# A planned attention and mixture kernel: the order of all queues made anew with other durations

## The chip, the cores and the metric

The kernel runs on one core of a Trainium2 chip. The metric is the device time of one execution in microseconds (us); the time of a kernel is the median of its runs. The core has five engines that run queues of their own, each in its written order: TensorE (PE; PEld is its weight load), VectorE (DVE), ScalarE (ACT), GpSimd (POOL) and SyncE (SP), which here only issues transfers. An engine waits for another by semaphores.

## What is computed

An attention whose scores are cut at a threshold below the row's maximum, and behind it a soft mixture of experts over the 4608 tokens of the attention's output.

```python
batch, n_heads, seq, head_dim = (8, 8, 576, 64)          # attention
N, D, E, S_per_e, F = (4608, 512, 8, 4, 1024)            # mixture
...
scores = scale * np.matmul(q, k.transpose(0, 1, 3, 2))
thresh = np.max(scores, axis=-1, keepdims=True) - tau
scores = np.where(scores >= thresh, scores, -1000000000.0)
attn = np.exp(scores - max); attn = attn / (sum + 1e-09)
x = np.matmul(attn, v)                                   # tokens x 512
...
logits = x @ phi                                         # 32 slots
d = softmax of logits over the tokens; slot_input = d.T @ x
h = np.maximum(slot_input[e] @ w1[e], 0.0); slot_out[e] = h @ w2[e]
c = softmax of logits over the slots; out = c @ slot_out
```

## The kernel before

**The attention stage** works on 32 pairs of heads, four for each of eight batches. A pair has nine score tiles of 128 queries by 576 keys: four blocks of 128 queries for each head, and one tile with the 64 leftover queries of both. For each tile TensorE multiplies q and k (L603, the leftover tile L608) into one of four PSUM regions. VectorE negates and copies the scores to a buffer `ss` (one of four) and takes their maximum in the same instruction (L615, followed by a short read of its accumulator). ScalarE makes exponentials of `ss` (L625). GpSimd adds tau to the maximum, a threshold of 128 numbers (L628). VectorE masks the exponentials by comparing `ss` with the threshold, and sums each row (L631). TensorE transposes the masked tiles into PSUM (L514), and ScalarE drains these to `pTa` and `pTb` (L519). TensorE multiplies them with V (L724), again into PSUM, and ScalarE drains that to `xT`.

The row sums go their own way: GpSimd adds a small number to the nine (L654), VectorE inverts them (L656), TensorE transposes them (L660), ScalarE drains them (L663), and SP writes them to device memory and reads them back spread over 64 rows each, as `R` (L666, L668, L671). Then GpSimd multiplies `xT` by `R` (L735). GpSimd also scales the next pair's keys (L567). After four pairs a **batch** ends: the logits (L796), exponentials with sums (L810), and the weighted sum of the tokens (L854, L859), which VectorE adds up in `acc` (L866).

**The tail** runs the experts: the weights that were not loaded during the attention stage, 38 transfers of 512 KB, stream in as buffers come free (L494, L496), TensorE multiplies them (L1055, L1092), and at last each token's mixture is computed and written out (L1136 to L1154).

**The order.** `pair` and `dispatch` do not issue work, they record operations in the list `G` (`Order.add`): engine, planned duration in ns, a nominal place, what is read and written. `Order.plan` then plays the list through with these durations, engine by engine: an engine takes the first of its next eight operations, by nominal place, whose inputs have come and whose buffers are free. The nominal places are numbers of the table `TABLE`, one for each operation of a pair, of a batch, and of the first and last ones. `LAT`, `CROSS` and `SAME` are what the plan adds between an operation and one that needs it; `more` corrects that for transfers. VectorE's masking instruction is marked `port=True`, and the plan lengthens it by 0.4 of the time for which GpSimd is still busy. What the plan starts first is written first, so the plan sets each queue's order, but only the chip sets the times.

Of the kernel before, what the change touches and what calls it, by code (L numbers as in the profile page):

```python
# [20 lines left out]
SAME = {"PE": 0, "DVE": 127, "ACT": 143, "POOL": 0, "SP": 2100}  # L21
# [19 lines left out]
for _n, _v in (  # L41
    ("batch", [
        20.265, 14.265, 22.458, 9.009, 14.083, 17.552, 21.280, 18.242, 23.399, 15.876, 23.639, 23.042, 19.525, 25.170,
        24.800, 22.578, 20.491,
    ]),
    ("end", [
        422.116, 101.628, 414.958, 444.428, 399.691, 457.508, 321.760, 634.874, 20.930, 417.720, 326.651, 574.203, 281.359,
        409.111, 490.768, 521.489, 539.548, 449.024, 949.190, 840.896, 21.300, 23.130, 583.989, 164.080, 735.574, 648.733,
        100.559, 245.423, 250.790, 679.817, 606.604, 75.253, 282.537,
    ]),  # L50
    ("first", [
# [8 lines left out]
    ]),  # L60
    ("head", [
        -486.655, -149.150, -116.459, -124.700, -355.836, -124.560, -124.240, -390.508, -284.773,
    ]),
    ("last", [
# [6 lines left out]
    ]),  # L71
    ("new0", [
        15.072, 8.053, 29.690, 11.400, 11.400, 11.500, 11.500, 18.149,
    ]),
    ("new1", [
        0.767, 12.245, 29.710, 11.400, 11.400, 11.500, 11.500, 22.125,
    ]),
    ("new2", [
        0.909, 15.170, 28.520, 11.400, 11.400, 11.500, 11.500, 16.909,
    ]),  # L80
    ("new3", [
        13.266, 9.302, 27.910, 11.400, 11.400, 11.500, 11.500, 7.214,
# [32 lines left out]
    ]),  # L115
    ("soft", [
        271.203, 288.777, 241.601, 224.162, 194.540, 428.743,
    ]),
    ("sums", [
        19.392, 21.213, 16.986, 20.521,  # L120
# [243 lines left out]
def softmax_attention_soft_moe(  # L364
# [17 lines left out]
    nc = tc.nc  # L382
# [84 lines left out]
    G = Order(kinds)  # L467
# [14 lines left out]
    n = NPRE + NHOST  # L482
# [752 lines left out]
```

## Time and profile before

| what | us |
|---|---|
| median of 3 runs (lowest to highest) | 540.19 (537.8 to 540.97) |
| the profiled execution, its own time | 539.73 |
| span of the profile | 537.6 |
| TensorE busy, share of the span | 517.3, 96% |
| VectorE busy | 472.0, 88% |
| ScalarE busy | 436.7, 81% |
| GpSimd busy | 243.2, 45% |

A page of the profile gives busy times over the whole span. They mix the attention stage, to about 460 us, with the tail. A view by stretches separates the two, and a timeline has the start and the duration of each instruction; a row with a count joins instructions that follow each other. In the timeline one score multiplication is four records of TensorE. The ends of matmuls are modelled and overlap the next ones, so the distance from one start to the next tells more than a duration. In brackets stands how long the engine was idle before, and what ended it.

### The profile page before, as it was taken

How to read it: one execution, taken by the hardware profiler on the slowest of the kernel's cores; microseconds unless marked ns; L12 is line 12 of the kernel's file. 1: busy time of each engine (PE TensorE's matmuls, PEld its weight loads, DVE VectorE, ACT ScalarE, POOL GpSimd, SP SyncE). 2: the span in 40 equal slices, each digit the busy share in tenths (PEclk: the TensorE clock that was granted, in tenths of full speed). 3: DMA queues.
4: the chain of work that ended last, by engine and by line, in shares of the span. 5: the costliest groups of instructions: out<-in, count | busy, mean ns of one | idle time of the engine just before them, and what ended most of it. 6: DMA issues, size and time to landing. Idle time of an engine off the chain costs nothing. (4 is left out here: it accounts for less than half of the span.)

```text
span 537.6 us, 18151 instructions
## 1 busy us (share of the span) xinstructions
PE 517.3 (96%) x6886; PEld 345.8 (64%) x6886; DVE 472.0 (88%) x1307; ACT 436.7 (81%) x784; POOL 243.2 (45%) x413
## 2 busy tenths in 40 slices
PE   8999999999999999999999999999999999999890
PEld 6566666676676676766766667766766766643370
DVE  6999999999999999999999999999999999613192
ACT  3898998988998899889989999989988999611181
POOL 2544564366535464545444643655346635021030
PEclk9999999999999999999999999999999999999996
DMA  6467676667556654544334444443344332999498
GB/s 156 99 192 192 195 192 194 190 182 193 166 152 193 184 165 154 127 110 98 113 93 115 115 114 115 114 116 114 111 118 116 103 106 104 389 409 408 161 382 321
DMA packets 37890, 92.31 MB, mean 172 GB/s; under 512 B 6068, under 2 KB 15020, under 8 KB 37804
## 3 DMA queue, kind: packets, MB, share of 16 engines
q1 hardware_dynamic: 37484, 90.90, 55.5%
q8 instruction: 54, 0.88, 0.7%
q10 hardware_dynamic: 320, 0.26, 0.2%
q14 instruction: 32, 0.26, 0.2%
HBM read 81.56 MB, written 9.58 MB: 170 GB/s over the span
## 5 line engine op out<-in xcount | busy, mean ns | idle before, releaser
L628 POOL TENSOR_SCALAR small<-small 128x1 f32<-128x1 f32 x288 | 143.0, 502 | 199.4 <-DVE ss L615 183.0
L615 DVE TENSOR_SCALAR_CACHE_REDUCE ss<-ps 128x576 f32<-128x576 f32 x288 | 208.9, 752 | 6.8 <-issue 2.3
L631 DVE SCALAR_TENSOR_TENSOR p<-ss,small,p 128x576 f32<-128x576 f32 x256 | 206.1, 825 | 0.9 <-POOL small L628 0.3
L625 ACT ACTIVATE p<-ss,small 128x576 f32<-128x576 f32 x256 | 186.5, 775 | 9.6 <-DVE ss L615 8.4
L603 PE MATMUL ps<-k,q 64*128 64x288 f32 x1024 | 159.0, 423 | 1.0 <-POOL small L628 0.9
L603 PEld LDWEIGHTS ps<-k,q 64*128 64x128 f32 x1024 | 85.7, 188 | 21.4 <-DVE ss L615 3.4
L514 PE MATMUL ps<-ident,p 64*128 64x64 f32 x2304 | 95.5, 224 | 0.6 <-ACT pTb L519 0.2
L514 PEld LDWEIGHTS ps<-ident,p 64*128 64x128 f32 x2304 | 86.3, 138 | 13.0 <-DVE ss L615 1.3
L519 ACT COPY pTb<-ps 128x1024 f32<-128x1024 f32 (+1 forms) x96 | 82.8, 874 | 10.9 <-PE ps L514 10.4
L724 PE MATMUL ps<-pTb,vv 128*64 128x320 f32 x512 | 76.0, 439 | 0.0
L519 ACT COPY pTa<-ps 128x1024 f32<-128x1024 f32 x64 | 63.1, 1011 | 0.8 <-PE ps L514 0.5
L724 PE MATMUL ps<-pTa,vv 128*64 128x256 f32 x512 | 62.3, 385 | 0.1
L724 PEld LDWEIGHTS ps<-pTb,vv 128*64 128x64 f32 x512 | 33.9, 136 | 34.1 <-ACT pTb L519 3.2
L735 POOL TENSOR_TENSOR xT<-xT,R 128x576 f32<-128x576 f32 x31 | 50.1, 1615 | 10.1 <-DMA R<-rd 4.2
L724 PEld LDWEIGHTS ps<-pTa,vv 128*64 128x64 f32 x512 | 33.9, 136 | 21.9 <-ACT pTa L519 3.6
L519 ACT COPY xT<-ps 128x256 f32<-128x256 f32 (+1 forms) x62 | 24.7, 398 | 5.8 <-PE ps L724 5.8
L631 DVE SCALAR_TENSOR_TENSOR pL<-ss,small,pL 128x576 f32<-128x576 f32 x32 | 28.4, 887 | 0.0
L625 ACT ACTIVATE pL<-ss,small 128x576 f32<-128x576 f32 x32 | 25.2, 787 | 3.1 <-DVE ss L615 3.1
L1012 POOL TENSOR_TENSOR c<-lall,crow 128x512 f32<-128x512 f32 x9 | 9.3, 1044 | 37.7 <-PE ct L506 23.4
L654 POOL TENSOR_SCALAR small<-small 128x9 f32<-128x9 f32 x31 | 16.7, 538 | 15.2 <-DVE p L631 8.1
L567 POOL TENSOR_SCALAR k<-k,small 128x576 f32<-128x576 f32 x31 | 23.4, 754 | 0.0
L615 DVE DVE_READ_ACCUMULATOR ss<-ps 128x1 f32 x288 | 23.4, 81 | 0.0
(159 smaller groups left out, 528.3 us busy)
## 6 DMA issues: line engine op xcount, KB each, us to landing
w<-in_w SPq DMA_DIRECT2D x45, 512.0 KB
q<-in_qT SPq DMA_DIRECT2D x62, 288.0 KB
vv<-in_vt SPq DMA_DIRECT2D x32, 320.0 KB
host<-in_w SPq DMA_DIRECT2D x19, 512.0 KB
k<-in_kT SPq DMA_DIRECT2D x62, 144.0 KB
R<-rd SPq DMA_DIRECT2D x62, 144.0 KB
out<-host SPq DMA_DIRECT2D x9, 512.0 KB
out<-w SPq DMA_DIRECT2D x7, 512.0 KB
```

Source lines behind the costliest of these rows:

```text
L514: nc.tensor.transpose(out=s[:, g, c:c + 64], in_=ins[g], identity=ident[rows[g], rows[g]], tile_position=(64 * g, 0))
L519: G.add("ACT", 51 + 0.833 * n, nom, lambda: nc.scalar.copy(*io()), r, w)
L567: scaled = lambda e, c=slice(0, S): lambda: e.tensor_scalar(out=kt.t[:, c], in0=kt.t[:, c], scalar1=flag8, **one)
L603: nc.tensor.matmul(s.t[:, g, 0:HS], qt.t[rows[g], h, c * 128:(c + 1) * 128], kt.t[rows[g], h * HS:(h + 1) * HS], start=True, stop=True, ti ...
L615: dve(674, t + OFF['mx'], [s], [ss, nmx], lambda s=s, ss=ss, nmx=nmx: nc.vector.tensor_scalar(out=ss.t.rearrange("p (a k) -> p a k", a=2), ...
L625: G.add("ACT", 668, t + OFF['ex'], lambda sv=sv, nmx=nmx, view=view: nc.scalar.activation(view().rearrange("p (a k) -> p a k", a=2), sv(), ...
L628: pool(250, t + OFF['th'], lambda nmx=nmx, thr=thr: nc.gpsimd.tensor_scalar(out=thr.t, in0=nmx.t, scalar1=1.0, scalar2=pabs, op0=ALU.mult, ...
L631: fn=lambda sv=sv, thr=thr, view=view, at=at: nc.vector.scalar_tensor_tensor(out=view().rearrange("p (a k) -> p a k", a=2), in0=sv(), scal ...
L654: pool(292, t + OFF['ri'], lambda: nc.gpsimd.tensor_scalar(out=ri.t[:, 0:N9], in0=r.t, scalar1=1e-9, scalar2=1.0, op0=ALU.add, op1=ALU.mul ...
L724: nc.tensor.matmul(W.t[h * 64:(h + 1) * 64, a, o:o + p0.shape[-1]], vv.t[:, v0:v0 + 64], p0, start=(kb == 0), stop=(kb == 4), tile_positio ...
L735: G.add("POOL", 1140, u + 5.6, own=own, r=[R], w=[xT], fn=lambda: nc.gpsimd.tensor_tensor(out=xT.t, in0=xT.t, in1=R.t, op=ALU.mult))
L1012: nc.gpsimd.tensor_tensor(out=c4, in0=lall[:, rows].unsqueeze(2).to_broadcast([128, k, 4, NS]), in1=crow[:, rows].unsqueeze(2).unsqueeze(3 ...
```

## The change

No operation is added or removed. Six planned durations or waits are other numbers: GpSimd's multiplication (L735) 1460 ns for 1140; ScalarE's two exponentials with sums 450 and 370 for 260 and 207; SP's three writes of the row sums 310, 450 and 620 for 600 each; its two reads back 550 for 650, with `more` -1000 for -1500; and what the plan adds between two operations of SP that depend on each other, 3300 for 2100. All numbers of the table but a few are new. The 0.4 for the port stays.

```diff
-SAME = {"PE": 0, "DVE": 127, "ACT": 143, "POOL": 0, "SP": 2100}
+SAME = {"PE": 0, "DVE": 127, "ACT": 143, "POOL": 0, "SP": 3300}
...
     ("batch", [
-        20.265, 14.265, 22.458, 9.009, 14.083, 17.552, 21.280, 18.242, 23.399, 15.876, 23.639, 23.042, 19.525, 25.170,
...
+        18.302, 10.858, 22.929, 20.593, 20.846, 23.057, 21.280, 21.310, 24.957, 22.816, 22.335, 22.234, 21.154, 25.170,
...
     ("sums", [
-        19.392, 21.213, 16.986, 20.521,
+        22.198, 17.464, 28.328, 56.205,
...
                 G.add("ACT", 158, t + 3.3, own=own, r=[w], w=[rt], fn=lambda w=w: nc.scalar.copy(
                     rt.t[0:N9].rearrange("p (g q) -> p g q", g=2), w.t[0:N9, :, 0:64]))
                 for h in range(2):
-                    G.add("SP", 600, t + 3.4, own=own, r=[rt], w=[rd[0, h]], more=-2500, fn=lambda h=h: nc.sync.dma_start(
+                    G.add("SP", 310 + 140 * h, t + 3.4, own=own, r=[rt], w=[rd[0, h]], more=-2500, fn=lambda h=h: nc.sync.dma_start(
                         rd.t[h, 0:SM].rearrange("(c q) -> c q", c=4), rt.t[h * 4:h * 4 + 4]))
-                G.add("SP", 600, t + 3.4, own=own, r=[rt], w=[rd[1]], more=-2500, fn=lambda: nc.sync.dma_start(
+                G.add("SP", 620, t + 3.4, own=own, r=[rt], w=[rd[1]], more=-2500, fn=lambda: nc.sync.dma_start(
                     rd.t[:, SM:S].unsqueeze(0), rt.t[8:9].rearrange("o (h q) -> o h q", h=2)))
                 for g in range(2):
-                    G.add("SP", 650, t + 3.5, own=own, r=[rd], w=[R[g]], more=-1500, fn=lambda g=g: nc.sync.dma_start(
+                    G.add("SP", 550, t + 3.5, own=own, r=[rd], w=[R[g]], more=-1000, fn=lambda g=g: nc.sync.dma_start(
                         R.t[rows[g]], rd.t[g:g + 1].to_broadcast([64, S])))
             elif not late and h == 1:
                 G.skip(4)
 ...
-            G.add("POOL", 1140, u + 5.6, own=own, r=[R], w=[xT], fn=lambda: nc.gpsimd.tensor_tensor(
+            G.add("POOL", 1460, u + 5.6, own=own, r=[R], w=[xT], fn=lambda: nc.gpsimd.tensor_tensor(
                 out=xT.t, in0=xT.t, in1=R.t, op=ALU.mult))
...
-        for k, (o, n) in enumerate(((slice(0, 128), 260), (slice(128, 192), 207))):
+        for k, (o, n) in enumerate(((slice(0, 128), 450), (slice(128, 192), 370))):
             G.add("ACT", n, u + 1.6, own=sums, r=[wl, new["run"]], w=[d["exp"], PERS["dsum"]], fn=lambda o=o, k=k: nc.scalar.activation(
                 d.t[:, o], lone(wl)[:, o], AF.Exp, bias=new.t[:, 1:2], accum_out=dsum[:, k:k + 1]))
```

What the table does is seen in the built program. TensorE, around the first scores of a new pair (here keys `k_239`), behind the attention-times-V of the pair before; `p` are masked tiles, `ps` are PSUM regions. Before:

```order
L514 MATMUL ps_256<-ident,p_219 128x64 x2
L514 MATMUL ps_256<-ident,p_199 128x64 x2
L514 MATMUL ps_257<-ident,p_199 128x64 x16
L603 MATMUL ps_258<-k_239,q_243 128x288 x2
L603 MATMUL ps_255<-k_239,q_243 128x288 x2
L514 MATMUL ps_256<-ident,p_215 128x64 x16
L514 MATMUL ps_257<-ident,p_203 128x64 x16
L608 MATMUL ps_258<-k_239,q_243 64x288 x4
L603 MATMUL ps_255<-k_239,q_243 128x288 x2
L603 MATMUL ps_256<-k_239,q_243 128x288 x2
```

After:

```order
L514 MATMUL ps_256<-ident,p_219 128x64 x2
L514 MATMUL ps_256<-ident,p_199 128x64 x2
L514 MATMUL ps_255<-ident,p_203 128x64 x16
L603 MATMUL ps_257<-k_239,q_243 128x288 x2
L603 MATMUL ps_256<-k_239,q_243 128x288 x2
L603 MATMUL ps_258<-k_239,q_243 128x288 x2
L603 MATMUL ps_255<-k_239,q_243 128x288 x2
L514 MATMUL ps_257<-ident,pL_171 128x64 x10
```

Two runs of two scores with transposes and the leftover tile (L608) between became one run of four, over all four regions; the leftover tile stands later.

VectorE, some rows into the second pair of the third batch; `ss0` to `ss3` are the four score buffers. Before:

```order
L615 TENSOR_SCALAR ss0_183,small_68<-ps3_258 128x576
L631 SCALAR_TENSOR_TENSOR p21_199,small_68<-ss1_211,small_68,p21_199 128x576
L615 TENSOR_SCALAR ss1_211,small_68<-ps2_257 128x576
L631 SCALAR_TENSOR_TENSOR p22_215,small_68<-ss2_207,small_68,p22_215 128x576
L615 TENSOR_SCALAR ss2_207,small_68<-ps1_256 128x576
L631 SCALAR_TENSOR_TENSOR p23_203,small_68<-ss1_211,small_68,p23_203 128x576
```

After:

```order
L631 SCALAR_TENSOR_TENSOR p21_199,small_68<-ss3_187,small_68,p21_199 128x576
L615 TENSOR_SCALAR ss0_207,small_68<-ps1_256 128x576
L615 TENSOR_SCALAR ss3_187,small_68<-ps0_255 128x576
L631 SCALAR_TENSOR_TENSOR p23_211,small_68<-ss2_163,small_68,p23_211 128x576
L615 TENSOR_SCALAR ss2_163,small_68<-ps1_256 128x576
L631 SCALAR_TENSOR_TENSOR p22_203,small_68<-ss0_207,small_68,p22_203 128x576
```

Before, two L615 here write the buffer that the L631 just ahead has read (`ss1`, `ss2`); after, one does (`ss2`).

VectorE, at the end of that batch's first pair. Before:

```order
L631 SCALAR_TENSOR_TENSOR p22_215,small_68<-ss0_183,small_68,p22_215 128x576
L631 SCALAR_TENSOR_TENSOR p22_215,small_68<-ss3_163,small_68,p22_215 128x576
L615 TENSOR_SCALAR ss0_183,small_68<-ps2_257 128x576
L631 SCALAR_TENSOR_TENSOR p23_203,small_68<-ss2_207,small_68,p23_203 128x576
L631 SCALAR_TENSOR_TENSOR p23_203,small_68<-ss1_211,small_68,p23_203 128x576
```

After:

```order
L631 SCALAR_TENSOR_TENSOR p22_203,small_68<-ss0_207,small_68,p22_203 128x576
L631 SCALAR_TENSOR_TENSOR p23_211,small_68<-ss1_215,small_68,p23_211 128x576
L631 SCALAR_TENSOR_TENSOR p22_203,small_68<-ss2_163,small_68,p22_203 128x576
L631 SCALAR_TENSOR_TENSOR pL0_171,small_68<-ss3_187,small_68,pL0_171 128x576
L615 TENSOR_SCALAR ss0_207,small_68<-ps0_255 128x576
```

Four L631 now stand in a row. Such rows of four were one in the whole program and are nine.

## Rows read from the trace of the kernel before

**Rows 1.** The page: busy us, share of the span, instructions of each engine.

```profile
PE 517.3 (96%) x6886; PEld 345.8 (64%) x6886; DVE 472.0 (88%) x1307; ACT 436.7 (81%) x784; POOL 243.2 (45%) x413
```

**Rows 2.** By stretch: length, busy us of PE, PEld, DVE, ACT, POOL, clock, DMA.

```profile
20.00:60.00 40.00, 39.46 (x534) 26.93 (x534) 39.55 (x112) 35.98 (x61) 19.89 (x35) 1.00 0.59 164
...
240.00:300.00 60.00, 59.86 (x850) 41.46 (x848) 58.19 (x163) 54.08 (x99) 30.23 (x51) 1.00 0.45 115
```

**Rows 3.** Timeline of TensorE in the second batch: start us, duration us, what, records.

```profile
101.51 0.83 PE L514 MATMUL ps<-ident,p 64*128 64x64 f32 x20
102.18 1.67 PE L603 MATMUL ps<-k,q 64*128 64x288 f32 x12
103.69 0.47 PE L514 MATMUL ps<-ident,pL 64*128 64x64 f32 x10
...
108.43 0.66 PE L514 MATMUL ps<-ident,p 64*128 64x64 f32 x16
108.92 1.19 PE L603 MATMUL ps<-k,q 64*128 64x288 f32 x8
109.95 0.66 PE L514 MATMUL ps<-ident,p 64*128 64x64 f32 x16
110.54 1.84 PE L724 MATMUL ps<-pTb,vv 128*64 128x320 f32 x12
```

**Rows 4.** Timeline of TensorE: the logits of batches 2, 3, 4 and 8.

```profile
86.41 1.53 PE L796 MATMUL ps<-xT,phi_sb 128*32 128x128 f32 x64
142.84 1.53 PE L796 MATMUL ps<-xT,phi_sb 128*32 128x128 f32 x64
200.66 1.53 PE L796 MATMUL ps<-xT,phi_sb 128*32 128x128 f32 x64
...
427.81 1.53 PE L796 MATMUL ps<-xT,phi_sb 128*32 128x128 f32 x64
```

**Rows 5.** Timeline of VectorE: an L615 behind an L631 of the same buffer.

```profile
98.39 0.08 DVE L631 DVE_READ_ACCUMULATOR pL<-ss,small,pL 128x1 f32 x1
98.59 0.76 DVE L615 TENSOR_SCALAR_CACHE_REDUCE ss<-ps 128x576 f32<-128x576 f32 x1
99.27 0.08 DVE L615 DVE_READ_ACCUMULATOR ss<-ps 128x1 f32 x1
99.27 0.82 DVE L631 SCALAR_TENSOR_TENSOR p<-ss,small,p 128x576 f32<-128x576 f32 x1
```

**Rows 6.** Timeline of several engines at three places where GpSimd and an L631 meet.

```profile
109.60 1.14 DVE L631 SCALAR_TENSOR_TENSOR p<-ss,small,p 128x576 f32<-128x576 f32 x1
...
173.38 2.05 DVE L631 SCALAR_TENSOR_TENSOR pL<-ss,small,pL 128x576 f32<-128x576 f32 x1
173.42 1.40 POOL L735 TENSOR_TENSOR xT<-xT,R 128x576 f32<-128x576 f32 x1 [0.20 <-DMA R<-rd]
...
175.59 0.52 PE L514 MATMUL ps<-ident,pL 64*128 64x64 f32 x10 [0.76 <-DVE pL L631]
...
441.69 1.24 POOL L567 TENSOR_SCALAR k<-k,small 128x576 f32<-128x576 f32 x1
...
442.24 1.29 DVE L631 SCALAR_TENSOR_TENSOR p<-ss,small,p 128x576 f32<-128x576 f32 x1
```

**Rows 7.** Timeline of TensorE: a run of four scores, and what follows it.

```profile
443.12 2.46 PE L603 MATMUL ps<-k,q 64*128 64x288 f32 x16
...
445.40 0.47 PE L514 MATMUL ps<-ident,pL 64*128 64x64 f32 x10
```

**Rows 8.** One source line: count, ns least/median/most, first and last start.

```profile
L735 POOL TENSOR_TENSOR xT<-xT,R x31: 1402/1458/1938, 32.1 to 456.1; 128x576 f32<-128x576 f32 x31
```

**Rows 9.** Timeline near the beginning: the second pair's keys and its first scores.

```profile
15.31 0.73 POOL L567 TENSOR_SCALAR k<-k,small 128x576 f32<-128x576 f32 x1
...
16.80 0.60 PE L603 MATMUL ps<-k,q 64*128 64x288 f32 x2 [0.90 <-POOL small L628]
```

**Rows 10.** By stretch, as rows 2: the tail while weights load.

```profile
464.00:503.00 39.00, 38.57 (x448) 16.96 (x446) 9.79 (x35) 7.67 (x22) 5.63 (x21) 1.00 1.01 401
```

More of the change, by code (lines that the diff above doesn't have):

```diff
@@ L42 @@
     ("batch", [
-        20.265, 14.265, 22.458, 9.009, 14.083, 17.552, 21.280, 18.242, 23.399, 15.876, 23.639, 23.042, 19.525, 25.170,
-        24.800, 22.578, 20.491,
+        18.302, 10.858, 22.929, 20.593, 20.846, 23.057, 21.280, 21.310, 24.957, 22.816, 22.335, 22.234, 21.154, 25.170,
+        24.800, 26.493, 25.629,
     ]),
     ("end", [
-        422.116, 101.628, 414.958, 444.428, 399.691, 457.508, 321.760, 634.874, 20.930, 417.720, 326.651, 574.203, 281.359,
-        409.111, 490.768, 521.489, 539.548, 449.024, 949.190, 840.896, 21.300, 23.130, 583.989, 164.080, 735.574, 648.733,
@@ L49 @@
-        100.559, 245.423, 250.790, 679.817, 606.604, 75.253, 282.537,
+        301.862, 124.881, 561.835, 326.908, 282.443, 488.775, 203.147, 786.750, 20.930, 629.636, 84.039, 874.559, 430.695,
+        399.561, 811.773, 370.590, 728.139, 341.016, 1042.783, 587.554, 21.300, 23.130, 823.228, 97.206, 1287.503, 1073.630,
+        374.223, 289.576, 665.706, 1244.037, 1191.015, 400.282, 474.095,
     ]),
     ("first", [
[8 rows of a table removed]
[8 rows of a table added]
     ]),
     ("head", [
-        -486.655, -149.150, -116.459, -124.700, -355.836, -124.560, -124.240, -390.508, -284.773,
+        -467.603, -149.150, -24.974, -124.700, -435.660, -124.560, -124.240, -804.214, -510.213,
@@ L63 @@
     ]),
     ("last", [
[6 rows of a table removed]
[6 rows of a table added]
     ]),
     ("new0", [
-        15.072, 8.053, 29.690, 11.400, 11.400, 11.500, 11.500, 18.149,
+        -2.119, 9.625, 29.690, 11.400, 11.400, 11.500, 11.500, 14.554,
     ]),
     ("new1", [
-        0.767, 12.245, 29.710, 11.400, 11.400, 11.500, 11.500, 22.125,
+        8.351, 13.344, 29.710, 11.400, 11.400, 11.500, 11.500, 9.243,
     ]),
     ("new2", [
-        0.909, 15.170, 28.520, 11.400, 11.400, 11.500, 11.500, 16.909,
+        16.352, 12.163, 28.520, 11.400, 11.400, 11.500, 11.500, 0.814,
@@ L80 @@
     ]),
     ("new3", [
-        13.266, 9.302, 27.910, 11.400, 11.400, 11.500, 11.500, 7.214,
+        7.519, 11.154, 27.910, 11.400, 11.400, 11.500, 11.500, 4.909,
     ]),
     ("pair0", [
[6 rows of a table removed]
[6 rows of a table added]
     ]),
     ("pair1", [
[6 rows of a table removed]
[6 rows of a table added]
     ]),
     ("pair2", [
[6 rows of a table removed]
[6 rows of a table added]
     ]),
     ("pair3", [
[6 rows of a table removed]
[6 rows of a table added]
     ]),
     ("soft", [
-        271.203, 288.777, 241.601, 224.162, 194.540, 428.743,
+        317.283, 270.993, 516.784, 155.887, 694.551, 783.864,
     ]),
     ("sums", [
-        19.392, 21.213, 16.986, 20.521,
+        22.198, 17.464, 28.328, 56.205,
@@ L121 @@
     ]),
     ("sumsend", [
-        192.259, 178.027, 591.492, 458.793,
+        586.760, 390.095, 532.994, 498.283,
     ]),
```

76 rows, old and new, of the table TABLE are left out of this document.

## The prediction

> **What bounds the kernel now.** I read the page's busy times first, then the busy times by stretch, then the timeline of TensorE. The page gives TensorE 96% of the span and VectorE 88% [rows 1]. The stretches tell more: from 20 to 60 us VectorE is busy 39.55 of 40 us, and later it is busy 58.19 of 60 with TensorE at 59.86 and the granted clock at 1.00 throughout [rows 2]. So two queues are full at once. TensorE's busy time proves little by itself, since matmuls overlap; the distances between starts prove more. Two score multiplications (x8 in the timeline) take 1.03 us to the next start and three (x12) take 1.51, so one costs 0.48 and a run of them 0.06 on top. A transpose of 16 records takes 0.49 before a score run and 0.59 before an attention-times-V block, so leaving the form that scores and transposes share costs 0.10. A transpose of 20 right after such a block takes 0.67 where 20/16 of 0.49 is 0.61, so coming back costs 0.06 [rows 3]. The starts recur at just these distances nearly everywhere: TensorE issues without a pause, and its time is set by how much work it has and how often it changes form. The pace shows in the start of the logits (L796), one a batch: 56.43 us to the next, then 57.82, then four batches in 227.15, or 56.79 each [rows 4].
>
> After the last attention work the weights are the limit: from 464 to 503 us the DMA engines are busy over their whole time [rows 10]. The queue of SP around them stays as it is: the row sums of the last pair but one, their spreading, then the loads. A main stage that is shorter by some time starts them sooner by that time, and the end moves with them.
>
> **The change, part by part.** No instruction is added or removed in the main stage; the planner gets other durations and a new table, and so all queues stand in another order. I price what can be counted.
>
> *TensorE's changes of form.* Counted over the attention stage, the runs of score multiplications go from 142 to 138, the exits from that shared form from 88 to 80 (leftover scores now often stand right before an attention-times-V block), and the returns from 86 to 78. With the prices above: 4 x 0.06 + 8 x 0.10 + 8 x 0.06 = 1.5 us less. This lies on TensorE's own queue, which nothing covers; I take it whole.
>
> *GpSimd's multiplication, planned at 1.46 us instead of 1.14.* The trace has it 31 times, 1.402, 1.458 and 1.938 us long (least, median, most) [rows 8]. What it does to VectorE is plain: while it runs, a masking instruction (L631, 0.81 us elsewhere) that falls due does not finish: 1.14 us at 109.60, and 2.05 at 173.38, where the multiplication took 1.40 from 173.42 [rows 6]. At 173.38 TensorE then stood still 0.76 us for that result [rows 6]; this is the batch that took 57.82 instead of 56.79, so 1.03 lost. It is not part of the pattern that repeats from batch to batch, but came where GpSimd ran off its plan. With the measured duration in the plan I take it away: 1.0 us. The bounds are 0 (another takes its place) and, on top of the 1.0, all that the batches lose against the shortest one: 8 x (56.79 - 56.43) = 2.9.
>
> The Trainium skill ("SBUF — State Buffer", section "Who interferes with whom") has this as an exclusive lock of a shared port pair: whoever starts first holds it for its whole instruction. The rows at 173 agree (0.81 + 1.24 = 2.05, of 1.40). It speaks against the change, since the planner, after it as before, charges VectorE only 0.4 of the overlap: by the 0.4 the new places of (b) below would cost 0.4 x 5.7 = 2.3 us, by the lock, as the rows have it, 5.7.
>
> *VectorE's queue.* Three things move. (a) A maximum instruction (L615) that stands right behind the L631 that read the same buffer waits for that to drain: it starts 0.20 us after the L631's last part began, 98.39 to 98.59, where otherwise the next starts at once [rows 5]. There are 29 such places before and 16 after: 13 x 0.20 = 2.6 us less. (b) In the written order, 7 of the 31 multiplications stand where one L615 and then an L631 follow (the 1.14 us case, 0.33 too long); after it are 14: 7 x 0.33 = 2.3 more. The scaling of the keys (L567) stands between L631 in a row once before, at 441.69, where L631 took 1.29 at 442.24 [rows 6], and 8 times after: 1.29 - 0.81 = 0.48, so 7 x 0.48 = 3.4 more, 5.7 together. (c) The stray stall at 173.38, 2.05 - 0.81 = 1.2, goes. Sum: -2.6 + 5.7 - 1.2 = +1.9 us. The bounds are -2.6 - 1.2 = -3.8 (the new places do not collide) and +3.1 (the stray stays). VectorE gains no room, so TensorE's gain can be used only as far as VectorE keeps up; most of these stalls did not reach TensorE before, whose starts stayed regular [rows 3], so I count none of them in the forecast.
>
> *Longer runs of scores.* Runs of four go from 2 to 23. The fourth needs the fourth PSUM region, which ScalarE must have drained; the run at 443.12, behind that stalled L631, is the only one in the steady stage of before. It took 2.28 us to the next start where 0.06 + 4 x 0.48 = 1.98 were due [rows 7]: 0.30 lost. A run of three shows no loss [rows 3]. In the new order the drain of that region stands, in two places of three, right behind two short drains with no exponential between them, so I take 0 (nearest to the run of three) and keep 0.30 each as the other bound.
>
> *The beginning.* TensorE idles 0.90 us at 16.80 until GpSimd has scaled the next keys (15.31) [rows 9]. In the new order that scaling stands one L628 earlier. But VectorE is full from there to 60 us [rows 2], so the gain is between 0 and 0.9; I take 0.
>
> *Small transfers and exponentials with sums.* Their new durations only move others; their instructions are the same and none ends a wait on TensorE in the rows. The transfers of row sums are planned nearer to each other on SP; they gate GpSimd's multiplication alone. I take 0. At the end the last multiplication stands behind the last L628 as before, and the last L631 behind both, so I take no change there.
>
> **Sum.** 1.5 + 1.0 = 2.5 us less. The profiled execution took 539.73 us, 0.46 below the median of 540.19 of three; from the median I forecast 540.2 - 2.5 = **537.7 us**. A measurement of this kernel can tell about 0.5%, 2.7 us, from no change.
>
> **Rivals.** *All waits of TensorE go.* Besides the 2.5: 2.9 for the batches and 0.9 at the beginning, together 6.3: 533.9 us. For it: the repeating waits are short and the plan now has their causes right. Against it: VectorE has no room for it [rows 2].
>
> *VectorE is the bound.* Then TensorE's changes of form are hidden and the sum is VectorE's: +1.9, so 542.1 us, no change that can be told. For it: 39.55 of 40 us in the first stretch [rows 2] and the new collisions. Against it: TensorE's starts without a pause [rows 3]. The Trainium skill ("Perfetto Trace Analysis", section "Identifying the Most-Contended Engine") judges TensorE by the weight loads' share and not by the matmuls'; that share is 64% [rows 1], and by that rule this rival would hold. The rows of starts speak against it.
>
> *The runs of four stall.* This ends slower. Place: the fourth score of a run waits for ScalarE, as at 443.12. Price: 21 more runs x 0.30 = 6.3 us; with the 1.5 for the form kept and the 1.0 not: 540.2 + 6.3 - 1.5 = 545.0 us. It eats the forecast's gain from 2.5 / 21 = 0.12 us a run, and makes the kernel slower by over 0.5% from (2.5 + 2.7) / 21 = 0.25. Against it: the drains stand close together now.
>
> **How the numbers follow.** Forecast 0.47, spread over 535.5 to 540, half of it beyond 0.5%; all waits go 0.18; VectorE is the bound 0.18; the runs of four stall 0.17. Faster by over 0.5%: 0.235 + 0.18 = 0.42. Within 0.5%: 0.235, nearly all of VectorE's 0.18 and a little of the slow case, 0.43. Slower: 0.15. The range reaches down to 533.0, for the case where all waits go, and up to 543.5, which takes in VectorE's case with its bound (540.2 + 3.1) and the milder half of the slow one; below and above that lies no more than 0.2.
>
> **What would show it.** Right: the starts of L796 lie 56.2 to 56.6 us apart with no batch near 57.8; the distance from a run of four to the next start is 1.98; places with 0.20 between L631 and L615 are 16. VectorE's rival shows in TensorE waiting for L631 or L615 in each batch. The slow rival shows in weight loads of L603 waiting for drains (L519). The forecast is wrong if the batches keep 56.8, or if the new collisions of L567 with L631 (1.29 us) push TensorE in each batch.

## The result, and the profile after

The changed kernel is slower: 547.12 us, median of 6 runs (545.04 to 547.90), against 540.24 of 6 (537.78 to 540.97) of the kernel before on the same chip, a ratio of 1.0133 (95% interval 1.0101 to 1.0165). The forecast was 537.7 and the range ended at 543.5. The profiled execution took 547.9 us, with a span of 545.9.

The page's busy times, as [rows 1]:

```profile
PE 519.1 (95%) x6886; PEld 348.4 (64%) x6886; DVE 480.4 (88%) x1307; ACT 441.1 (81%) x784; POOL 244.1 (45%) x413
```

The busy times by stretch, columns as in [rows 2]:

```profile
20.00:60.00 40.00, 39.19 (x524) 26.43 (x522) 39.37 (x112) 37.24 (x63) 19.70 (x34) 1.00 0.58 160
240.00:300.00 60.00, 59.15 (x840) 40.93 (x838) 58.80 (x166) 54.34 (x99) 31.31 (x51) 1.00 0.40 103
120.00:180.00 60.00, 57.81 (x798) 40.30 (x796) 54.89 (x154) 52.17 (x93) 28.17 (x48) 0.97 0.57 170
```

TensorE's busy time hardly differs, and VectorE's is 8.4 us longer. But TensorE is no longer without a gap: 59.15 of 60 us where it was 59.86 [rows 2], and from 120 to 180 us 57.81, with VectorE at 54.89. So something holds both now. The pace says where. The starts of L796 in the first six of the eight batches, as [rows 4] (whose four rows are the first, second, third and seventh batch), from the timeline of TensorE:

```profile
87.28 1.53 PE L796 MATMUL ps<-xT,phi_sb 128*32 128x128 f32 x64
147.79 1.53 PE L796 MATMUL ps<-xT,phi_sb 128*32 128x128 f32 x64
206.11 1.53 PE L796 MATMUL ps<-xT,phi_sb 128*32 128x128 f32 x64
263.12 1.53 PE L796 MATMUL ps<-xT,phi_sb 128*32 128x128 f32 x64
321.40 1.53 PE L796 MATMUL ps<-xT,phi_sb 128*32 128x128 f32 x64
379.69 1.53 PE L796 MATMUL ps<-xT,phi_sb 128*32 128x128 f32 x64
```

The steps are 60.51, 58.32, 57.01, 58.28 and 58.29 us, where the kernel before had 56.43, 57.82 once and 56.8 to 56.9 else. 57.0 is the undisturbed step now, and four of the five are longer by 1.3 or 3.5.

What ends the new waits, from the table of waits: engine, what waited and for what, total us, times, longest. First the kernel before, then after:

```profile
POOL xT L735 <- DMA R<-rd: 4.2, 7, 1.3
PEld ps L514 <- POOL xT L735: 0.4, 1, 0.4
```

```profile
PEld ps L514 <- POOL xT L735: 7.0, 7, 1.9
POOL xT L735 <- DMA R<-rd: 5.4, 6, 1.4
PE ps L514 <- POOL xT L735: 5.0, 4, 1.8
DVE p L631 <- POOL small L628: 2.0, 4, 1.5
```

TensorE (PE, 5.0 us in four places; its weight loads, PEld, in seven) waits for GpSimd's multiplication, which it almost never did before. One of the four places, in the timeline of SP, GpSimd and TensorE (start, duration, what; in brackets the idle time before it and what ended it), after:

```profile
184.05 0.27 SPq L666 DMA_DIRECT2D rd<-rt  x1
...
185.03 0.41 SPq L666 DMA_DIRECT2D rd<-rt  x1
185.72 0.51 SPq L585 DMA_DIRECT2D q<-in_qT  x1
186.33 1.79 SPq L559 DMA_DIRECT2D k<-in_kT  x2
188.18 0.59 SPq L585 DMA_DIRECT2D q<-in_qT  x1
...
188.94 1.11 SPq L671 DMA_DIRECT2D R<-rd  x2
...
194.27 1.78 POOL L735 TENSOR_TENSOR xT<-xT,R 128x576 f32<-128x576 f32 x1 [1.30 <-DMA R<-rd]
...
196.11 0.46 PE L514 MATMUL ps<-ident,xT 64*128 64x64 f32 x8 [1.06 <-POOL xT L735]
```

and the same place before:

```profile
179.41 0.27 SPq L666 DMA_DIRECT2D rd<-rt  x1
...
181.45 0.51 SPq L585 DMA_DIRECT2D q<-in_qT  x1
182.05 1.62 SPq L559 DMA_DIRECT2D k<-in_kT  x2
183.84 1.12 SPq L671 DMA_DIRECT2D R<-rd  x2
185.64 0.47 SPq L585 DMA_DIRECT2D q<-in_qT  x1
187.93 1.75 POOL L735 TENSOR_TENSOR xT<-xT,R 128x576 f32<-128x576 f32 x1
...
190.68 0.46 PE L514 MATMUL ps<-ident,xT 64*128 64x64 f32 x8
```

This is the way back of a pair's row sums, here of the fourth pair of a batch (there are seven such places; the recorded expectations call it the second head): three small transfers (L666, L668), two copies that spread them over the partitions (L671), the multiplication (L735), TensorE's transposes of its result. Before, the second half of the next q (L585, 288 KB) is issued behind the two copies; after, ahead of them. From the first small transfer to the multiplication it took 8.52 us before (187.93 - 179.41) and takes 10.22 now. Before, TensorE came to the transposes 1.00 us after the multiplication had ended (189.68 to 190.68): there was that much room and no more. Now it stands still 1.06 us there. In the 60.51 us batch it waits 1.79 us, and that multiplication also holds GpSimd's next instruction, for which VectorE then idles 1.53 us:

```profile
134.33 1.82 POOL L735 TENSOR_TENSOR xT<-xT,R 128x576 f32<-128x576 f32 x1 [2.00 <-DVE p L631]
136.14 0.50 POOL L628 TENSOR_SCALAR small<-small 128x1 f32<-128x1 f32 x2
...
136.21 0.46 PE L514 MATMUL ps<-ident,xT 64*128 64x64 f32 x8 [1.79 <-POOL xT L735]
136.43 0.82 DVE L631 SCALAR_TENSOR_TENSOR p<-ss,small,p 128x576 f32<-128x576 f32 x1 [1.53 <-POOL small L628]
```

(The timeline puts the 2.00 us down to an L631 that started at 133.34 and took 0.82 us, so it ended at 134.16. The chain of waits has the row sums there: a copy issued at 128.37 that took 5.80 us, and so ended at 134.17.)

The 3.5 us of that batch are not all waiting. Behind this stop of TensorE the granted clock, 1.00 from 20 to 60 and from 240 to 300 us, fell to 0.50 (1.2 GHz of 2.4); a stretch, with its columns as in [rows 2], and two rows of TensorE inside it:

```profile
137.40:140.70 3.30, 3.30 (x29) 2.52 (x26) 1.53 (x4) 2.55 (x6) 0.99 (x2) 0.50 0.32 94
```

```profile
137.61 1.07 PE L514 MATMUL ps<-ident,p 64*128 64x64 f32 x16
138.47 2.81 PE L603 MATMUL ps<-k,q 64*128 64x288 f32 x12
```

The same two rows took 0.66 and 1.67 us at the full clock [rows 3], so about 1.5 of the 3.5 us are the clock's. The clock over the whole span was 0.988 in this execution and 0.990 to 0.992 in the other five, of which two took as long (547.38 and 547.87), so this fall need not be in the median.

Two theories can explain the waits. **A:** the row sums' way back is late, through SP's new order. **B:** the new places of GpSimd's instructions beside L631, on the port that it shares with VectorE, cost the time.

### The profile page after: what moved, and what is told of

It reads as the page before. It is cut to its first block, busy times and chain, and to the rows that moved or that the text cites. A ratio compares the mean times of both kernels' runs of the same rounds, so it can differ in the third digit from the quotient of the medians.

```text
span 545.9 us, 18106 instructions
## 1 busy us (share of the span) xinstructions
PE 519.1 (95%) x6886; PEld 348.4 (64%) x6886; DVE 480.4 (88%) x1307; ACT 441.1 (81%) x784; POOL 244.1 (45%) x413
## 4 chain that ended last, share of the span: by engine, by line
PE 59%; DVE 11%; issue 10%; DMA 9%; ACT 4%; POOL 3%; SPq 2%; DVEq 0%; POOLq 0%; ACTq 0%
PE ps L724 18%; PE ps L603 18%; PE ps L514 13%; DVE ss L615 5%; DMA w<-in_w 4%; DMA R<-rd 4%; DVE p L631 3%; PE ps L796 2%; PE h L1055 2%; PE ps L608 2%; ACT p L625 1%; POOL xT L735 1%; PE ps L854 1%; DVE pL L631 1%; ACT pTa L519 1%
## 5 line engine op out<-in xcount | busy, mean ns | idle before, releaser
L628 POOL TENSOR_SCALAR small<-small 128x1 f32<-128x1 f32 x288 | 145.7, 511 | 207.1 <-DVE ss L615 197.2
L631 DVE SCALAR_TENSOR_TENSOR p<-ss,small,p 128x576 f32<-128x576 f32 x256 | 218.1, 876 | 2.0 <-POOL small L628 2.0
L615 DVE TENSOR_SCALAR_CACHE_REDUCE ss<-ps 128x576 f32<-128x576 f32 x288 | 209.6, 748 | 10.8 <-ACT pTb L519 4.1
L603 PE MATMUL ps<-k,q 64*128 64x288 f32 x1024 | 161.1, 426 | 0.7 <-DVE k L567 0.3
L603 PEld LDWEIGHTS ps<-k,q 64*128 64x128 f32 x1024 | 89.1, 189 | 22.1 <-ACT pTa L519 3.6
L514 PE MATMUL ps<-ident,p 64*128 64x64 f32 x2304 | 98.4, 224 | 0.3 <-ACT pL L519 0.2
L514 PEld LDWEIGHTS ps<-ident,p 64*128 64x128 f32 x2304 | 88.3, 139 | 10.9 <-DVE ss L615 2.3
L735 POOL TENSOR_TENSOR xT<-xT,R 128x576 f32<-128x576 f32 x31 | 53.5, 1727 | 16.9 <-ACT xT L519 8.0
L567 POOL TENSOR_SCALAR k<-k,small 128x576 f32<-128x576 f32 x31 | 27.0, 870 | 0.0
L631 DVE SCALAR_TENSOR_TENSOR pL<-ss,small,pL 128x576 f32<-128x576 f32 x32 | 26.0, 814 | 0.0
L615 DVE DVE_READ_ACCUMULATOR ss<-ps 128x1 f32 x288 | 23.3, 81 | 0.0
L608 PE MATMUL ps<-k,q 64*64 64x288 f32 x256 | 23.0, 427 | 0.0
```

The source lines that it names most:

```text
L514: nc.tensor.transpose(out=s[:, g, c:c + 64], in_=ins[g], identity=ident[rows[g], rows[g]], tile_position=(64 * g, 0))
L567: scaled = lambda e, c=slice(0, S): lambda: e.tensor_scalar(out=kt.t[:, c], in0=kt.t[:, c], scalar1=flag8, **one)
L603: nc.tensor.matmul(s.t[:, g, 0:HS], qt.t[rows[g], h, c * 128:(c + 1) * 128], kt.t[rows[g], h * HS:(h + 1) * HS], start=True, stop=True, ti ...
L608: nc.tensor.matmul(s.t[rows[a], g, 0:HS], qt.t[rows[g], a, SM:S], kt.t[rows[g], a * HS:(a + 1) * HS], start=True, stop=True, tile_position ...
L615: dve(674, t + OFF['mx'], [s], [ss, nmx], lambda s=s, ss=ss, nmx=nmx: nc.vector.tensor_scalar(out=ss.t.rearrange("p (a k) -> p a k", a=2), ...
L628: pool(250, t + OFF['th'], lambda nmx=nmx, thr=thr: nc.gpsimd.tensor_scalar(out=thr.t, in0=nmx.t, scalar1=1.0, scalar2=pabs, op0=ALU.mult, ...
```

## Experiments: what is late, and why

All ratios are to the kernel before in runs on the same chip, with 95% intervals.

**The second half of q behind the copies again.** Only these seven places of SP's queue change; every other queue is the changed kernel's.

After the plan is made, the starts of these transfers are exchanged. This edit and the others of its kind are shown shortened (`sp` is SP's order, `loads` the indices of the loads of q and of the copies):

```diff
 start, slot = self.plan(TABLE)
+for x, y, z in zip(sp, sp[1:], sp[2:]):
+    if x in loads["q"] and y in loads["R"] and z in loads["R"]:
+        start[x] = start[z] + .01
```

> The changed kernel with one edit: in the second head of the seven batches from the fourth multiplication on (seven places), the load of the second half of q, which the new order issues ahead of the two copies that bring the row sums back (L671), is issued behind them. All other queues are as in the changed kernel. Theory A (the row sums' way back is late: q in front of L671 makes the multiplication on GpSimd, L735, start late, and TensorE's transposes of its result wait): the waits of 1.8, 1.1, 1.1 and 1.1 us ahead of these transposes (136.21, 196.11, 311.44, 369.73) shrink to under 0.3 us each, and with what they trail (batch steps 60.5 and 58.3 against 57.0) the time falls by 4 to 7 us, to 540-543. Theory B (the new places of L735 and L567 beside L631 on the shared port cost it, whenever the sums come): within 1.5 us of the changed kernel, 545.5-548.

Measured: 541.37 us, ratio 1.0038 (1.0019 to 1.0057). Some 5 of the 7 us lost are back by one transfer in seven places. Two waits of TensorE are left (1.8 us together, one of them 1.1), where the copies were late all the same: from the issue of the first to the landing of the second they took 6.22 and 5.67 us, where the other six fourth pairs have 4.2 in the mean. Nothing here shows why.

**The same edit the other way, in the kernel before.**

```diff
 start, slot = self.plan(TABLE)
+for n, x in enumerate(sp[:-3]):
+    if x in loads["R"][6::8] and sp[n - 2] in loads["q"]:
+        for q in sp[n + 2:n + 4]:
+            if q in loads["q"]:
+                start[q] = start[x] - .01
```

> The kernel before with the same edit the other way round: in the second head of seven batches the second half of q is issued ahead of L671 instead of behind it, all other queues as before. Theory A: the copies land about 0.8 to 2 us later, L735 starts that much later, the 1.0 us that TensorE's transposes leave after L735 is used up in most of these places, and the time rises by 1 to 6 us, to 541-546. Theory B: 539.5-541.5, since no place of L735 or L567 is moved by the plan.

Measured: 545.57 us, ratio 1.0122 (1.0101 to 1.0143). The kernel before, which has none of the new places of GpSimd, becomes as slow as the changed one by this transfer alone. GpSimd's and TensorE's waits in its table:

```profile
POOL xT L735 <- DMA R<-rd: 14.8, 11, 2.5
PE ps L514 <- POOL xT L735: 4.3, 6, 1.0
```

A is shown in both directions; the new places of B can't be what makes the difference between the two kernels. But late sums act in two ways. In four of the seven places TensorE waits 0.96 to 0.98 us; in the other three it waits under 0.3 us, and the late multiplication starts ahead of an L631, which then takes 1.74 to 1.99 us. The two of these that lie between logits have batches as much longer as the rest (57.88 and 57.70 us, of 56.88 and 56.73 before).

**The copies first.** In the changed kernel L671 stands straight behind the small transfers, so neither k nor q is ahead of it.

In the diff `m` is the last small transfer ahead of the first copy `x`:

```diff
 start, slot = self.plan(TABLE)
+for n, x in enumerate(sp):
+    if x in loads["R"][0::2]:
+        start[x], start[sp[n + 1]] = start[m] + .001, start[m] + .002
```

> The changed kernel with the row sums' copies (L671) issued straight behind the three small transfers that they wait for, in all heads, so that no load of k or q stands between them. Other queues as in the changed kernel. Theory A: L735 never starts late for the sums, the batch steps are all near 57.0, 539.5-542.5. Theory B: 545.5-548. If the loads of k and q, pushed back by 2 to 3 us, are now late themselves, the time lies above the run with only q behind.

Measured: 540.39 us, ratio 1.0020 (1.0006 to 1.0035). No wait of TensorE for L735 is left, and L796 starts 56.9 to 57.0 us apart throughout.

**Is it q's bytes or its place in the queue?** The same instructions in the same order as in the changed kernel, but in the seven places the half of q ahead of the copies moves 36 of the 576 columns of each head, a sixteenth of its bytes.

```diff
-nc.sync.dma_start(qt.t[rows[g]], qT[b, j])
+nc.sync.dma_start(qt.t[rows[g], :, 0:36], qT[b, j, :, :, 0:36])
```

> The changed kernel with its own queues, where the second half of q that stands ahead of L671 (seven places) moves a sixteenth of its bytes (36 of 576 columns of each half, so the scores of these heads are partly of old columns). Theory A1 (it is q's 288 KB, in flight ahead of the sums, that hold them up): near the run with q behind, 540.5-542.5, and the copies land under 4.2 us after the first of them is issued (4.8 to 6.3 with the whole q). Theory A2 (it is the place in SP's queue, 0.75 us): 545 or more, landing as late as in the changed kernel.

Measured: 541.83 us, ratio 1.0048 (1.0025 to 1.0070), with 0.2 us of TensorE's waiting left. So the place alone costs little: without most of its bytes q hardly holds anything up. Worked out from the issues and the semaphores' events of the seven places: from the issue of the first copy to the landing of the second it takes 5.21 us in the mean in the changed kernel (4.73 to 6.33), 4.27 with q cut, 4.32 in the kernel before. The bound of 4.2 us that I had set for each of them did not hold (3.47 to 5.00). So q ahead of the copies made them later by its place (it is issued 0.76 us ahead of them) and by 0.9 us through its bytes, against 1.00 us of room in the place shown; whether the bytes without the place would also do it is not shown. The Trainium skill ("DMA: Bandwidth & Descriptors", section "Queues, rings and completion order") has descriptors consumed in the order of their ring; that a transfer issued 0.76 us earlier makes the next ones land 0.9 us later agrees with it.

**Which edit put q there?** The planner takes L671 as ready a fixed time after the transfer that it waits for (SAME of SP). The change raises it from 2100 to 3300 ns, and whatever else has arrived is issued in the meantime. The changed kernel with that number put back, and nothing else:

```diff
-SAME = {"PE": 0, "DVE": 127, "ACT": 143, "POOL": 0, "SP": 3300}
+SAME = {"PE": 0, "DVE": 127, "ACT": 143, "POOL": 0, "SP": 2100}
```

> The changed kernel with one number of the planner put back: the time from one transfer to the next that waits for it (SAME of SP) 2100 instead of 3300; the table and all other durations are the new ones. The plan then puts the second half of q behind L671 by itself in the second heads, but it also moves other rows, since the table was searched for 3300. If the 3300 is what costs the time (theory A): 539.5-543. If the rest of the new order costs it: 545 or more.

Measured: 540.00 us, ratio 1.0019 (0.9999 to 1.0039), L796 56.5 us apart in five of six batches. The new table, planned with the old number, has no loss left that can be told. In this run q stands ahead of the copies in the third pairs instead (0.67 to 1.01 us ahead, the copies landing in 4.2 to 4.8), and it costs nothing there: the multiplication still ends 1.9 to 2.6 us before TensorE comes to its transposes. So it is the room that decides. The other way round, the kernel before with 3300:

> The kernel before, with its table and durations, and this one number of the planner changed: 3300 instead of 2100 for the wait between dependent transfers. The plan puts the second half of q ahead of L671 in the second and the third heads, and vv in the first heads. Theory A: slower than before by as much as or more than the run with q ahead in the second heads alone (545.6): 545-550. If a whole plan makes up for it elsewhere: 540-543.

Measured: 563.31 us, ratio 1.0443 (1.0402 to 1.0485): worse than I expected, with 6.3 us of TensorE waiting for L735 and steps of 59 to 62 us. How long the wait is in truth can be read where nothing stands between. Timeline of SP, kernel before:

```profile
193.21 0.41 SPq L666 DMA_DIRECT2D rd<-rt  x1
194.66 1.12 SPq L671 DMA_DIRECT2D R<-rd  x2
```

From the end of the last small issue (193.62) to the copy's issue are 1.04 us, half of the old number and a third of the new. Planned with that:

> The changed kernel planned with the wait between dependent transfers that the trace shows where nothing stands between them (1.03 us from the end of the last small transfer's issue to the issue of L671): 1030 instead of 3300. The plan puts L671 ahead of k in every head, and one half of q ahead of it in the second heads. The table was searched for another number, so rows move on all engines. Theory A: no waits of TensorE for the multiplication of over 0.5 us, 538-541.5. If the order is bad in another way for it: up to 544.

Measured: 557.33 us, ratio 1.0329 (1.0300 to 1.0359), a plain miss. TensorE waits for the multiplication no more, but steps are 57.6 to 59.9: the measured number, beside a table that was searched for another one, gives yet another order. I did not take this run's order apart, so why it is slow is not shown.

## Experiments: what the multiplication costs beside L631

**No gate at all.** In the changed kernel the multiplication reads its own operand twice and so waits for no sums (the division by the row sums is left out).

> The changed kernel with the multiplication on GpSimd reading its own operand twice instead of the row sums, so that nothing waits for the sums' way back (the division by the row sums is left out of the computation); the transfers are still issued. Theory A: 539-542.5, the same as with the sums first, and no wait of TensorE for L735 but where xT itself is late. Theory B: 545-548, since the multiplication lies beside L631 all the same. In between, both.

Measured: 538.26 us, ratio 0.9979 (0.9966 to 0.9992). This is under both expected ranges and 2.1 us under the run with the copies first, in which no wait of TensorE for the sums was left either. So the 2.1 us need not be the gate's: with one operand the multiplication itself takes 1.15 us alone instead of 1.41, and lies beside L631 for less time.

**No multiplication.** L735 is left out (the division is not computed), first in the changed kernel, then in the kernel before:

```diff
-            G.add("POOL", 1460, u + 5.6, own=own, r=[R], w=[xT], fn=lambda: nc.gpsimd.tensor_tensor(
-                out=xT.t, in0=xT.t, in1=R.t, op=ALU.mult))
+            G.add("POOL", 1460, u + 5.6, own=own, r=[R], w=[xT], fn=lambda:
+                None)
```

> The changed kernel without the multiplication on GpSimd (L735 left out, so the division by the row sums is not computed); its transfers and all other queues stay. Against the run in which the multiplication reads its own operand (538.26) this takes away its time beside L631 too. Theory B's share (the shared port): L735 lengthens L631 by about 16 us in VectorE's queue together with L567; if a quarter of that reaches the end, 533.5-536. If VectorE's cover is as large as I took it to be in the prediction (nothing reaches the end): 537.5-538.5.

> The kernel before without L735, as the control. If the new order is better by the prediction's 2.5 us once nothing waits for the sums and nothing meets on the port, this lies 2 to 3 us above the changed kernel without L735; if the new order is no better in itself, within 1 us of it. By the one stray collision (1.03 us of TensorE at 173.38) it should lie at least 1 us under the kernel before: at most 538.3.

Measured: 535.23 us, ratio 0.9943 (0.9921 to 0.9964), and 535.84 us, ratio 0.9942 (0.9924 to 0.9961). Two things follow. The multiplication costs the kernel before some 3.0 us (538.82 - 535.84), and the changed kernel with its copies first some 0.77% or 4.2 us (1.0020 - 0.9943). TensorE hardly waits for it in either, so I put this down to the meetings on the port; what GpSimd's freed time is worth is not told apart. B is a real cost, but nearly the same in both. And with gate and port out of the way the new order is better by 0.6 us by the medians and not at all by the ratios, where I expected 2 to 3.

**The copies first in the kernel before.** This was to change nothing.

> The kernel before with the row sums' copies (L671) issued straight behind the small transfers that they wait for, other queues as before. Theory A: TensorE waited 0.4 us for L735 in all there, so nothing is to be had: 538.5-540, ratio 0.997 to 1.001, unless L735, which then starts earlier by up to 1.3 us, meets L631 elsewhere (0.3 to 1 us either way).

Measured: 543.93 us, ratio 1.0086 (1.0064 to 1.0107), a miss, and the most useful one. No wait for the sums is left, and yet it lost 5 us. The timeline at a third pair of a batch (the recorded texts say third head), first in the kernel before, then with the copies first:

```profile
230.42 0.75 DVE L615 TENSOR_SCALAR_CACHE_REDUCE ss<-ps 128x576 f32<-128x576 f32 x1
...
231.10 0.81 DVE L631 SCALAR_TENSOR_TENSOR pL<-ss,small,pL 128x576 f32<-128x576 f32 x1
...
231.84 0.75 DVE L615 TENSOR_SCALAR_CACHE_REDUCE ss<-ps 128x576 f32<-128x576 f32 x1
231.87 1.41 POOL L735 TENSOR_TENSOR xT<-xT,R 128x576 f32<-128x576 f32 x1 [0.94 <-DMA R<-rd]
```

```profile
231.72 0.75 DVE L615 TENSOR_SCALAR_CACHE_REDUCE ss<-ps 128x576 f32<-128x576 f32 x1
...
232.19 1.41 POOL L735 TENSOR_TENSOR xT<-xT,R 128x576 f32<-128x576 f32 x1
232.40 1.82 DVE L631 SCALAR_TENSOR_TENSOR pL<-ss,small,pL 128x576 f32<-128x576 f32 x1
```

Before, the late sums happened to start the multiplication here beside two L615, which it doesn't touch (0.75 us each). Earlier sums start it 0.21 us ahead of an L631, which then takes 1.82 instead of 0.81. Two causes were left: this meeting (C), or the loads of k and q, pushed back by 2 us (D). Four runs tell them apart. Without the multiplication, with the loads where they are:

> The kernel before with the sums' copies first and without the multiplication (the division by the row sums is left out). Theory C: the same as without the multiplication alone (535.8), 535-537. Theory D: 540 or more.

Measured: 535.40 us, ratio 0.9930 (0.9910 to 0.9950): the 5 us are the multiplication's, and D is out. With two small instructions ahead of it in the third pairs, so that it starts later:

```diff
+idle = lambda: nc.gpsimd.tensor_scalar(out=pad, in0=pad, scalar1=1.0, scalar2=1.0, op0=ALU.mult, op1=ALU.add)
+for i in loads["m"][2::4]:
+    ops[i] = ops[i][:2] + (lambda f=ops[i][2]: (idle(), idle(), f()),) + ops[i][3:]
```

> The kernel before with the sums' copies straight behind the small transfers, and two instructions of one column (0.27 us each) on GpSimd ahead of the multiplication in the third heads, so that it starts about 0.5 us later. Theory C (543.9 came from the multiplication starting 0.2 us ahead of an L631, which then took 1.82 us): it starts inside that L631 again, steps near 56.5, 537.5-540. Theory D (the loads of k and q, pushed back): 543-545.

Measured: 537.61 us, ratio 0.9966 (0.9946 to 0.9986), faster than both kernels, with the steps of L796 at 56.4 to 56.8 throughout. The same place in it:

```profile
229.99 0.81 DVE L631 SCALAR_TENSOR_TENSOR pL<-ss,small,pL 128x576 f32<-128x576 f32 x1
230.72 0.75 DVE L615 TENSOR_SCALAR_CACHE_REDUCE ss<-ps 128x576 f32<-128x576 f32 x1
230.81 1.41 POOL L735 TENSOR_TENSOR xT<-xT,R 128x576 f32<-128x576 f32 x1
```

The two small instructions took 1.06 us, twice what I had expected, and the multiplication starts just as that L631 ends, not inside it. One microsecond of doing nothing in the third pair of each batch is worth 6.3 us here (543.93 to 537.61, by the ratios 1.2%). The changed kernel with its copies first, and with 2100 and the copies first, did not profit:

> The changed kernel with the sums' copies first and the same two small instructions ahead of the multiplication in the third heads. There L735 starts 0.20 us ahead of an L631 that then takes 1.83 us. Theory C: L631 at 0.81 in these heads, the steps fall from 56.94 by 0.3 to 0.5, 537-539. Theory D, or TensorE's transposes waiting for the later multiplication (0.8 us were left): 540-542.

Measured: 541.96 us, ratio 1.0050 (1.0032 to 1.0069). L631 is at 0.82 in these pairs, but the multiplication, now started 0.10 us behind one, waits for it and takes 1.99, and TensorE's transposes wait:

```profile
235.13 0.82 DVE L631 SCALAR_TENSOR_TENSOR p<-ss,small,p 128x576 f32<-128x576 f32 x1
235.23 1.99 POOL L735 TENSOR_TENSOR xT<-xT,R 128x576 f32<-128x576 f32 x1
...
237.28 0.46 PE L514 MATMUL ps<-ident,xT 64*128 64x64 f32 x8 [0.78 <-POOL xT L735]
```

The rival that I had named for it holds: only 0.8 us were left there.

> The changed kernel planned with 2100 instead of 3300 for the wait between transfers, and besides with the row sums' copies straight behind the small transfers. With 2100 alone the batch steps were 56.5 (before 56.7 to 57.7) and two waits of TensorE for the multiplication were left (0.56 us in all). Theory A: the waits go, 537.5-539.5, a shade faster than the kernel before. Theory C (learnt from the kernel before with its sums first, 543.9: a multiplication that starts earlier can meet L631 instead of a pair of L615): steps of 57 or more and 541-544.

Measured: 543.59 us, ratio 1.0077 (1.0048 to 1.0107), with steps of L796 of 57.5 in four of six batches and 56.5 in two. In the four the third pair's multiplication makes an L631 take 1.95 us, in the two it holds none up. So C, not A, again.

> The changed kernel planned with 2100, the sums' copies first, and the small instructions ahead of the multiplication in the third heads. Without them five of its seven steps were 57.5 and one 56.5, the one where L735 met no L631. Theory C: all near 56.5, 536.5-539. Theory D: 543 as without them.

Measured: 544.24 us, ratio 1.0096 (1.0066 to 1.0125), a miss (without the small instructions four of six steps were at 57.5, as given above, and so they are here): the multiplication waits there for ScalarE's copy of xT (12.2 us over 13 places), which hides the two small instructions, and it starts where it started before.

## Why the prediction was wrong, point by point

- **Small transfers, "they gate GpSimd's multiplication alone. I take 0."** This is the step that failed, with nearly all of the loss behind it. The multiplication gates TensorE's transposes, 1.00 us behind it in the place shown, and the prediction has no row of that distance; its rows of L735 [rows 6, 8] are about what it does to VectorE. It also has the transfers "planned nearer to each other", where the raised number plans the copies 1.2 us further from the small transfers (3300 for 2100 ns), and it is in this time that q was put ahead of L671. The prediction has no word of q. Price by the runs: 5 to 6.6 us (q put behind: 1.0133 to 1.0038; q put ahead in the kernel before: 1.0122). "None ends a wait on TensorE in the rows" was true of the rows before and says nothing of how near a wait is.
- **The stray meeting at 173.38, -1.0.** The 57.82 us batch was that, as I had it: in the kernel before with copies first and multiplication later the same batch takes 56.75. But the bound "another takes its place" is what happened in the changed kernel: in all seven third pairs an L631 took 1.82 to 1.97 us, and 1.83 still in its run with the copies first.
- **VectorE's queue, +1.9, "I count none of them".** The counts hold (16 places of 0.20 us; the scaling of the keys makes an L631 1.29 us long in each batch), but not that they stay in VectorE's queue. In the kernel before with the copies first, the L631 that the multiplication meets in the third pairs is 1.01 us longer (1.82 - 0.81) and the batch 0.9 (steps of 57.5 against 56.6 with the multiplication later). VectorE has no cover for such a place. The Trainium skill ("SBUF — State Buffer", section "Who interferes with whom"), which the prediction weighed against the planner's 0.4, has the later one fully blocked; the rows agree, both for L631 (1.82 us) and for the multiplication (1.99 us). The row at 173.38, which the prediction read as agreeing, doesn't by its recorded starts: L631 starts 0.04 us ahead of the multiplication there and is the one that waits [rows 6]. The sum was also too small: on the two pages L631's busy time grew by 9.6 us (206.1 us for `p` and 28.4 for `pL` before, 218.1 and 26.0 after), where (b) and (c) make 4.5. Of what reached the end, the runs without the multiplication show its share alone: 3.0 us before and 4.2 after with the copies first, and the 1.2 between them is within the noise of the ratios. No run prices the meetings of L567 or the 16 places.
- **TensorE's changes of form, -1.5.** The mechanism may hold, though no run isolates it; the gain at the end isn't there. Without the multiplication, from the first logits to the seventh (six batches) the new order takes 338.07 us and the old 339.36, so 1.29 less; but the first logits come 0.80 later (86.87 and 86.07), where the prediction's term for the beginning was 0 with a gain as its only other bound, and the medians differ by 0.6.
- **Runs of four, 0 with 0.30 as the bound.** Near enough. One a batch loses something: 84.52 to 86.69 is 2.17 where 1.98 were due, so 0.19, or 1.3 us over seven batches.

```profile
84.52 2.34 PE L603 MATMUL ps<-k,q 64*128 64x288 f32 x16
86.69 0.66 PE L514 MATMUL ps<-ident,p 64*128 64x64 f32 x16
```

- **The rivals.** The one that came nearest in time, runs of four (545.0), did so by luck: its runs lose 1.3 of its 6.3 us. None had a result that comes late from outside VectorE and TensorE. "The batches keep 56.8" was named as what would show the forecast wrong; they went to 57.0 and more.

What stays open: why the plan with 1030 is so much worse, why the copies landed late in two places of the run with q behind them, and how the 1.1 us (ratio 1.0020) by which the changed kernel with its copies first stays above the kernel before are made up; the 1.2 us more that the multiplication costs there would cover them, but no run parts them.

## What to carry to other kernels

Before a step is called free because it "only" gates an idle engine, follow it on to the busy engine that takes its result, and read the distance there. A table of waits has only the places where that distance is already used up. Here 1.00 us was not room for a transfer of 288 KB put ahead of a dependent one; where there was more, as in the third pairs of the run with 2100, it cost nothing. A plan by measured durations is only as good as the number for each wait in the context where it stands, and a table searched with one set of numbers can't be run with another: one constant moved the time by between 1% and 4%. Where two engines meet on a port, the moment of the start decides; an earlier result can cost more than a late one.

## What the runs showed of the hardware that I had not expected

- A multiplication on GpSimd that starts 0.21 us ahead of an L631 makes that take 1.82 us instead of 0.81; one that starts 0.10 us behind it takes 1.99 itself, of 1.41; one that starts beside two L615 costs neither anything (1.41 and 0.75).
- The two copies of 144 KB landed 4.3 us after the issue of the first in the mean, and 5.2 us with another 288 KB issued 0.76 us ahead of them; the longest took 6.3.
- A transfer could be issued 1.04 us after the issue of the small one that it waits for had ended.
- Behind a stop of TensorE of 1.79 us (to 136.21) the granted clock was 0.50 from 137.40 to 140.70 us, and in the kernel before with 3300, behind one of 1.92 us (to 320.64), from 321.50 to 324.80.
